# One PSUM tile per bank, another start order and filler matmuls in a fused attention and channel-mix kernel

## The chip, the cores and the metric

The kernel runs on one core of a Trainium2 chip. The metric is the device time of one execution in microseconds (us), lower is better. A profile is one execution, taken beside the timed ones. PE is the matrix engine, ACT the scalar engine, DVE the vector engine, POOL is GpSimd, SP the sync engine.

## The reference

Eight batches, eight heads, 576 positions, head size 64. Linear attention comes first, then a channel mix with d_model 512 and d_ff 1024:

```
q_s = softmax(q over d);  k_s = softmax(k over positions)
x   = q_s @ (k_s^T @ v)              # per batch and head, then heads side by side: [8, 576, 512]
xk  = mu_k*x + (1-mu_k)*x_prev       # x_prev is x, one position earlier
xr  = mu_r*x + (1-mu_r)*x_prev
out = sigmoid(xr @ w_r) * (relu(xk @ w_k)^2 @ w_v)
```

## The kernel before

The kernel plans itself. It lists operations with an estimated length, a sort key and dependencies, orders them in a small simulation, and writes the instructions in that order. Each engine then runs its own list strictly in order and waits on semaphores. The semaphores are not set by the planner but by the framework, from the tiles that the instructions read and write.

PSUM has eight banks of 128 x 512 f32. The kernel before takes them as four tiles of two banks. The planner, however, hands out six slots: two pairs ("att") and four single banks ("mm"):

```python
banks = [psum.tile([128, 2, 512], F32, name=f"bank_{x}") for x in "abcd"]
ps = {"mm": [banks[2 + i // 2][:, i % 2, :] for i in range(4)],
      "att": [t[:, :, :] for t in banks[0:2]], "early": [t[:, :, :] for t in banks[2:4]]}
```

So mm slots 0 and 1 are the two halves of tile bank_c, and slots 2 and 3 those of bank_d. The steady work is in units of 512 columns. Each unit has 8 wk groups, and for each 128 columns an r group and two v groups, all in mm slots (four 512-column matmuls each):

```python
# K: 4 matmuls into a mm slot, then ACT relu, then DVE square -> k2
# R: 4 matmuls into a mm slot, then ACT tanh -> th
# V: 8 matmuls (two groups of 4) into a mm slot, then DVE (th + 1) * v -> ot, then a store
# ... (cut)
o = plan.add("PE", 0.864, 1.03, clock, lambda v=v_part: v(range(4, 8)),
             squares[4:8] + [o] + wv_done[1:2], [], [k2])
```

The data of a V group come from DVE (the squares) and from wv, never from ACT.

The start: batch 0's q, k, v come on the SP and ACT queues, weights and all other batches on POOL's queue. Batch 0 is mixed on PE with masked weights built from mu:

```python
gate = [first[GATE]]                 # the first wk load waits for one of batch 0's loads
# ... (cut)
mask_zeros = plan.add("POOL", 2.2, 2.3, -7, emit_mask_zeros)
# mu_rows: two loads on ACT's queue per mu; mask copies: 4 DVE instructions per mu
```

The softmax here doesn't subtract the row's maximum and nothing guards it: scores larger than these inputs give would overflow.

## Time and profile before

| | before |
|---|---|
| median of 3 runs | 230.28 us |
| span of the profiled execution | 228.7 us |
| first transposes of q | 11.49 us |
| first wk matmul | 22.63 us |
| unit 1's first r matmul | 60.16 us |
| last matmul ends | 224.07 us |

The page's lines for span and busy time of each engine:

```profile
span 228.7 us, 3591 instructions
PE 196.1 (86%) x1281; PEld 98.1 (43%) x1281; DVE 164.9 (72%) x368; ACT 152.3 (67%) x228; POOL 41.6 (18%) x65
```

PE is the busiest engine. Its columns alone, at the steady rate of 0.86 us for four 512-column matmuls, come to about 190 us, so roughly 38 us of the span are not PE work. The timeline of the first 24 us shows one part. Its columns are start, length, engine, line, operation, output<-input, shapes, count, and in brackets the idle time before it and its releaser:

```profile
5.75 1.25 ACT L399 ACTIVATE eq_a<-raw_a 128x576 bf16<-128x576 f32 x2 [1.23 <-DMA raw_a<-in_q_dram]
8.44 1.42 DVE L413 TENSOR_REDUCE rsum_a<-eq_a 128x9 f32<-128x576 bf16 x2
...
11.49 1.14 PE L443 MATMUL bank_a<-ident,qs_a 128*128 128x128 bf16 x9 [2.75 <-DVE qs_a L421]
...
16.30 1.17 PE L496 MATMUL bank_a<-qt_a,wp_a 128*128 128x512 bf16 x5
...
22.63 1.44 PE L617 MATMUL bank_c<-xk,wk_bf 128*128 128x512 bf16 x4
...
23.91 0.66 PE L496 MATMUL bank_b<-qt_a,wp_b 128*128 128x512 bf16 x5
```

PE waits 11 us for a chain load, exp, row sum, scale. The same five mixing matmuls take 1.17 us at 16.30 and 0.66 us at 23.91, so PE runs at half rate until about then. Below, "cold" means matmuls at this half rate and "warm" at the full one, always read from their lengths.

The other part is spread over the steady stretch. The view of waits lists what ended PE's idle time there (releaser: us in total, times, longest); these are five of its eight lines for 60 to 120 us:

```profile
PE bank_d L617 <- DVE ot_c L664: 1.2, 1, 1.2
PE bank_c L658 <- ACT th_b L653: 1.0, 1, 1.0
PE bank_d L617 <- ACT rel_b L602: 0.8, 1, 0.8
PE bank_d L617 <- ACT rel_a L602: 0.7, 1, 0.7
PE bank_d L658 <- ACT rel_a L602: 0.7, 1, 0.7
```

From 60 us to the end such lines add to 8.4 us in 15 waits (the view lists waits above 0.15 us). They look like ordinary waits for a free PSUM slot. The second one is not, and the timeline around it shows why (L648 is an r group, L658 a v group, th_b a tanh):

```profile
86.48 1.03 PE L648 MATMUL bank_c<-wr_bf,xr 128*128 128x512 bf16 x4
87.34 1.03 PE L658 MATMUL bank_d<-wv_bf,k_a 128*128 128x512 bf16 x4
88.72 0.61 ACT L653 ACTIVATE th_b<-bank_c 128x512 f32<-128x512 f32 x1
...
89.38 1.02 PE L658 MATMUL bank_c<-wv_bf,k_a 128*128 128x512 bf16 x4 [1.02 <-ACT th_b L653]
```

The r group at 86.48 fills one half of bank_c. ACT reads it with th_b only at 88.72, having been busy. The v group that follows wants the other half of bank_c, which nobody uses, and still waits until the tanh is done.

### The profile page before, as it was taken

What the parts mean: (1) busy time and instruction counts of PE and PEld (TensorE: products, weight loads), DVE (VectorE), ACT (ScalarE), POOL (GpSimd) and SP (SyncE); (2) the same over time, 40 slices, a digit from 0 to 9 for tenths busy, and PEclk for the clock granted to TensorE, in tenths of its full rate; (3) what the DMA queues carried; (4) which work ended last, traced back from release to release, by engine and by line L of the source; (5) the groups of instructions that cost most, each with busy time, mean ns of one, the idle gap of its engine ahead of it and who ended that gap; (6) DMA issues with size and microseconds to landing.
All of it is one profiled execution on the core that took longest, in us unless ns stands there. A gap on an engine that the chain in (4) does not pass through costs nothing. (4 is left out here: it accounts for less than half of the span.)

```text
span 228.7 us, 3591 instructions
## 1 busy us (share of the span) xinstructions
PE 196.1 (86%) x1281; PEld 98.1 (43%) x1281; DVE 164.9 (72%) x368; ACT 152.3 (67%) x228; POOL 41.6 (18%) x65
## 2 busy tenths in 40 slices
PE   0076999967899878998979999999999999999881
PEld 0053444533354434543446544444543454444530
DVE  1774855898899959989787989699578538832521
ACT  2658689798898688587427897957775664452430
POOL 8615437344322122112000000000000000000000
PEclk9999999999999999999999999999999999999999
DMA  6999999999999858868372040222042122403404
GB/s 199 299 292 357 209 338 390 402 399 402 393 400 404 290 193 232 237 159 268 109 195 46 4 92 0 64 63 62 0 94 67 25 49 46 92 0 91 94 3 92
DMA packets 16722, 40.88 MB, mean 179 GB/s; under 512 B 2360, under 2 KB 5184, under 8 KB 16704
## 3 DMA queue, kind: packets, MB, share of 16 engines
q0 software_dynamic: 8896, 27.40, 37.3%
q1 hardware_dynamic: 7200, 12.39, 20.1%
q10 hardware_dynamic: 608, 0.85, 1.2%
q8 instruction: 10, 0.16, 0.3%
q14 instruction: 8, 0.07, 0.1%
HBM read 33.82 MB, written 9.44 MB: 189 GB/s over the span
## 5 line engine op out<-in xcount | busy, mean ns | idle before, releaser
L617 PEld LDWEIGHTS <-wk_bf 128*128 128x128 bf16 x320 | 30.6, 98 | 39.0 <-issue 9.9
L617 PE MATMUL bank_d<-xk,wk_bf 128*128 128x512 bf16 (+1 forms) x160 | 37.1, 357 | 3.5 <-DVE ot_c L664 1.2
L617 PE MATMUL bank_c<-xk,wk_bf 128*128 128x512 bf16 (+1 forms) x160 | 37.6, 360 | 2.3 <-ACT rel_a L602 1.6
L658 PEld LDWEIGHTS <-k_a 128*128 128x128 bf16 x144 | 13.5, 97 | 18.9 <-issue 3.0
L658 PE MATMUL bank_c<-wv_bf,k_a 128*128 128x512 bf16 x80 | 20.2, 379 | 1.3 <-ACT th_b L653 1.0
L658 PEld LDWEIGHTS <-k_b 128*128 128x128 bf16 x144 | 13.5, 97 | 17.5 <-issue 3.1
L648 PEld LDWEIGHTS <-xr 128*128 128x128 bf16 x144 | 13.3, 98 | 17.3 <-issue 2.4
L658 PE MATMUL bank_d<-wv_bf,k_b 128*128 128x512 bf16 x80 | 20.2, 379 | 0.3 <-DVE ot_b L664 0.3
L648 PE MATMUL bank_c<-wr_bf,xr 128*128 128x512 bf16 x72 | 18.5, 379 | 0.8 <-ACT rel_c L602 0.6
L648 PE MATMUL bank_d<-wr_bf,xr 128*128 128x512 bf16 x72 | 18.5, 379 | 0.5 <-ACT th_b L653 0.5
L658 PE MATMUL bank_d<-wv_bf,k_a 128*128 128x512 bf16 x64 | 16.1, 379 | 1.6 <-DVE ot_c L664 0.9
L658 PE MATMUL bank_c<-wv_bf,k_b 128*128 128x512 bf16 x64 | 16.2, 379 | 1.2 <-DVE ot_b L664 0.8
L602 ACT ACTIVATE rel_c<-bank_d 128x512 bf16<-128x512 f32 (+1 forms) x17 | 9.3, 547 | 8.7 <-PE bank_d L617 8.1
L602 ACT ACTIVATE rel_b<-bank_c 128x512 bf16<-128x512 f32 (+1 forms) x17 | 9.5, 559 | 5.9 <-PE bank_c L617 5.2
L653 ACT ACTIVATE th_a<-bank_c 128x512 f32<-128x512 f32 x10 | 6.0, 598 | 7.3 <-PE bank_c L648 3.4
L602 ACT ACTIVATE rel_a<-bank_c 128x512 bf16<-128x512 f32 (+1 forms) x14 | 7.5, 539 | 4.0 <-PE bank_c L617 3.8
L653 ACT ACTIVATE th_a<-bank_d 128x512 f32<-128x512 f32 x8 | 4.8, 599 | 6.4 <-PE bank_d L648 5.7
L602 ACT ACTIVATE rel_a<-bank_d 128x512 bf16<-128x512 f32 (+1 forms) x13 | 7.4, 570 | 1.8 <-PE bank_d L617 1.6
L606 DVE TENSOR_TENSOR k_a<-rel_b 128x512 bf16<-128x512 bf16 (+1 forms) x14 | 5.6, 404 | 3.9 <-ACT rel_b L602 3.7
L443 PE MATMUL bank_a<-ident,qs_a 128*128 128x128 bf16 x72 | 5.8, 230 | 2.8 <-DVE qs_a L421 2.8
L447 ACT COPY qt_a<-bank_a 128x1152 bf16<-128x1152 bf16 x5 | 5.6, 1117 | 3.7 <-PE bank_a L443 3.7
L653 ACT ACTIVATE th_b<-bank_c 128x512 f32<-128x512 f32 x8 | 4.8, 598 | 4.8 <-PE bank_c L648 4.5
(208 smaller groups left out, 389.0 us busy)
## 6 DMA issues: line engine op xcount, KB each, us to landing
out_dram<-ot_a SPq DMA_DIRECT2D x24, 128.0 KB, 2.4
out_dram<-ot_b SPq DMA_DIRECT2D x24, 128.0 KB, 2.4
out_dram<-ot_c SPq DMA_DIRECT2D x24, 128.0 KB, 2.4
raw_a<-in_q_dram POOLq DMA_DIRECT2D x3, 576.0 KB, 8.7
raw_b<-in_q_dram POOLq DMA_DIRECT2D x3, 576.0 KB, 7.0
raw_c<-in_k_dram POOLq DMA_DIRECT2D x3, 576.0 KB, 7.7
raw_d<-in_v_dram POOLq DMA_DIRECT2D x3, 576.0 KB, 8.5
raw_e<-in_k_dram POOLq DMA_DIRECT2D x3, 576.0 KB, 9.7
```

What stands on the lines that cost most here:

```text
L443: nc.tensor.transpose(out=transposed()[:, j, :], in_=qss[qs.index][:, j, :], identity=ident[:])
L447: nc.scalar.copy(out=qts[qt.index][:], in_=transposed()[:, 0:J, :])
L602: nc.scalar.activation(out=rels[rel.index][:, 0:n], in_=bank(kf)[:, 0:n], func=ACT.Relu, scale=HALF_ROOT)
L606: nc.vector.tensor_tensor(out=k2s[k2.index][:, fc, 0:n], in0=rels[rel.index][:, 0:n], in1=rels[rel.index][:, 0:n], op=ALU.mult)
L617: nc.tensor.matmul(bank(kf)[:, 0:n], lhsT=wk_bf[:, ct, fc * 128:(fc + 1) * 128], rhs=xs[0][:, ct, c0:c0 + n], start=(ct == 0), stop=(ct == ...
L648: nc.tensor.matmul(bank(rps), lhsT=xs[1][:, ct, c:c + 128], rhs=wr_bf[:, ct, :], start=(ct == 0), stop=(ct == CT - 1))
L653: nc.scalar.activation(out=ths[th.index][:], in_=bank(rps), func=ACT.Tanh, scale=0.5)
L658: nc.tensor.matmul(bank(vps), lhsT=k2s[k2.index][:, ft, 128 * m:128 * m + 128], rhs=wv_bf[:, ft, :], start=(ft == 0), stop=(ft == FT - 1))
```

## The change

The intent is to take false waits out of PSUM and to shorten the start. The PSUM part, with `kv_of` picking the single bank where the first batch's k^T v used a pair:

```diff
-    banks = [psum.tile([128, 2, 512], F32, name=f"bank_{x}") for x in "abcd"]
-    ps = {"mm": [banks[2 + i // 2][:, i % 2, :] for i in range(4)],
-          "att": [t[:, :, :] for t in banks[0:2]], "early": [t[:, :, :] for t in banks[2:4]]}
+    ps = {"mm": [psum.tile([128, 512], F32, name=f"mm_{x}") for x in "abcd"],
+          "att": [psum.tile([128, 2, 512], F32, name=f"att_{x}") for x in "ab"]}
+    def kv_of(slot, hf):
+        if slot.pool == "early":
+            return ps["mm"][2 * slot.index + hf][:]
+        return bank(slot)[:, hf, :]
```

The start part, cut to its core:

```diff
-                if closed:
+                if closed and not op.size:          # loads keep the order they are given
-    mask_zeros = plan.add("POOL", 2.2, 2.3, -7, emit_mask_zeros)      (on GpSimd)
+    mask_zeros = plan.add("DVE", 1.8, 1.9, 0, emit_mask_zeros)        (on DVE)
-            nc.scalar.dma_start(            # mu_rows
+            nc.gpsimd.dma_start(
-            nc.vector.tensor_copy(out=mu_mask...); nc.vector.tensor_scalar(...)
+            nc.gpsimd.tensor_copy(out=mu_mask...); nc.gpsimd.tensor_scalar(...)
+    def filler(slot):
+        for _ in range(2):
+            nc.tensor.matmul(bank(slot)[:, 0:128], lhsT=ident[:], rhs=ident[:], start=True,
+                             stop=True)
+    for _ in range(FILL):                   # FILL = 40
+        slot = Slot("mm")
+        plan.add("PE", 0.11, 0.2, 2 * LATE, lambda slot=slot: filler(slot), [identity], [slot],
+                 [slot])
(cut: some lengths and keys that the planner uses, and a reciprocal split in two)
```

The first line has a consequence that the diff hides: batch 0 now loads as q, q, k, v, and the gate of the weights, unchanged in the text, now falls on the v of the first head group, the last of its loads. In the kernel before that v was issued first, so the gate opened at once.

More of the change, by code (lines that the diff above doesn't have):

```diff
@@ L34 @@
 GATE = 7
-MU_KEY = (0.5, 1.9, LATE, LATE)
+FILL = 40
 ON_PE = (0,)
@@ L233 @@
     ots = buffers("ot", [128, C], F32)
-    banks = [psum.tile([128, 2, 512], F32, name=f"bank_{x}") for x in "abcd"]
-    ps = {"mm": [banks[2 + i // 2][:, i % 2, :] for i in range(4)],
-          "att": [t[:, :, :] for t in banks[0:2]], "early": [t[:, :, :] for t in banks[2:4]]}
+    ps = {"mm": [psum.tile([128, 512], F32, name=f"mm_{x}") for x in "abcd"],
+          "att": [psum.tile([128, 2, 512], F32, name=f"att_{x}") for x in "ab"]}
     def bank(slot):
-        return ps[slot.pool][slot.index]
+        return ps[slot.pool][slot.index][:]
+    def kv_of(slot, hf):
+        if slot.pool == "early":
+            return ps["mm"][2 * slot.index + hf][:]
+        return bank(slot)[:, hf, :]
     xs = [const.tile([128, CT, RING], BF16, name=n) for n in ("xk", "xr")]
@@ L300, in emit_mask_zeros @@
     def emit_mask_zeros():
-        nc.gpsimd.memset(mu_mask[:].rearrange("p m s c e -> p (m s c e)"), 0.0)
+        nc.vector.memset(mu_mask[:].rearrange("p m s c e -> p (m s c e)"), 0.0)
     def emit_late_consts():
@@ L310 @@
     plan.add("ACT", 2.0, 2.0, 1.5, emit_warm, [zero])
-    mu_load = plan.add("POOL", 1.2, 1.2, -9, emit_mu_load, size=8.0)
-    identity = plan.add("POOL", 0.6, 0.8, -8, emit_identity)
-    consts = plan.add("DVE", 0.5, 0.6, -9, emit_consts, [identity])
+    mu_load = plan.add("POOL", 1.2, 1.2, -9.2, emit_mu_load, size=8.0)
+    identity = plan.add("POOL", 0.6, 0.8, -9.1, emit_identity)
+    consts = plan.add("DVE", 0.2, 0.3, -9, emit_consts, [identity])
     late_consts = plan.add("DVE", 0.6, 0.7, LATE, emit_late_consts)
-    mask_zeros = plan.add("POOL", 2.2, 2.3, -7, emit_mask_zeros)
+    mask_zeros = plan.add("DVE", 1.8, 1.9, 0, emit_mask_zeros)
     mu_slot = Slot("mm")
@@ L335, in emit_mu_mask @@
             r = slice(64 * u, 64 * u + 64)
-            nc.vector.tensor_copy(out=mu_mask[r, m, 0, :, r], in_=mu_rows[r, m, :, :])
-            nc.vector.tensor_scalar(out=mu_mask[r, m, 1, :, r], in0=mu_rows[r, m, :, :],
+            nc.gpsimd.tensor_copy(out=mu_mask[r, m, 0, :, r], in_=mu_rows[r, m, :, :])
+            nc.gpsimd.tensor_scalar(out=mu_mask[r, m, 1, :, r], in0=mu_rows[r, m, :, :],
                                     scalar1=-1.0, scalar2=1.0, op0=ALU.mult, op1=ALU.add)
     mu_t = plan.add("PE", 0.2, 0.4, -500, emit_mu, [mu_load, consts], [mu_slot])
-    mu_done = plan.add("DVE", 0.08, 0.17, LATE, emit_mu_copy, [mu_t], gives=[mu_slot])
+    mu_done = plan.add("DVE", 0.08, 0.17, 0, emit_mu_copy, [mu_t], gives=[mu_slot])
     mu_masked = []
     for m in range(2):
-        o = plan.add("ACT", 0.9, 0.9, MU_KEY[m], lambda m=m: emit_mu_rows_load(m), size=131.0)
-        mu_masked.append(plan.add("DVE", 1.0, 1.1, MU_KEY[2 + m], lambda m=m: emit_mu_mask(m),
+        o = plan.add("POOL", 1.4, 1.4, -9.5 + m, lambda m=m: emit_mu_rows_load(m), size=131.0)
+        mu_masked.append(plan.add("POOL", 1.6, 1.7, -2 + m, lambda m=m: emit_mu_mask(m),
                                   [o, mask_zeros]))
+    def filler(slot):
[6 more added lines that the diff above has]
+                 [slot])
     def weight_part(dst, src, n, u, c0, c1):
@@ L429, in kv @@
                     nc.tensor.matmul(
-                        bank(kvp)[:, hf, 0:129],
+                        kv_of(kvp, hf)[:, 0:129],
                         lhsT=eks[ek.index][r, j, :, :].rearrange("p u d -> p (u d)"),
@@ L434, in recz @@
         def recz():
-            nc.vector.reciprocal(out=rzs[rz.index][:, :, None],
-                                 in_=bank(kvp)[:, :, 128:129])
+            if kvp.pool == "att":
+                nc.vector.reciprocal(out=rzs[rz.index][:, :, None],
+                                     in_=bank(kvp)[:, :, 128:129])
+            else:
+                for hf in range(2):
+                    nc.vector.reciprocal(out=rzs[rz.index][:, hf:hf + 1],
+                                         in_=kv_of(kvp, hf)[:, 128:129])
         def transposed():
@@ L480, in attention @@
         kvm = plan.add("PE", 0.63, 0.7, pe_key, kv, expk + castv, [kvp], [ek, vv])
-        zdone = plan.add("DVE", 0.066, 0.15, step + 2, recz, [kvm], [rz])
+        zdone = plan.add("DVE", 0.08 * (2 if b == 0 else 1), 0.25 if b == 0 else 0.16, step + 2, recz, [kvm], [rz])
         def weights_of(wp, m, hf, s):
             nc.vector.scalar_tensor_tensor(
-                out=wps[wp.index][:, hf, s, :], in0=bank(kvp)[:, hf, 0:128],
+                out=wps[wp.index][:, hf, s, :], in0=kv_of(kvp, hf)[:, 0:128],
                 scalar=rzs[rz.index][:, hf:hf + 1], in1=mu_mask[:, m, s, 2 * g + hf, :],
@@ L571, in attention @@
                                 [xb] if hf == 0 else [], [xps[hf]]))
-        o = plan.add("DVE", 0.1, 0.19, step + 6, edge, evs)
+        o = plan.add("DVE", 0.11, 0.19, step + 6, edge, evs)
         xdiff = plan.add("DVE", 0.66, 0.755, step + 6, diff, [o], [xd])
```

## The prediction

> **What bounds the kernel now.** The page gives PE 86% busy, ACT 67%, DVE 72%. At the warm rate of the steady stretch (0.86 us per four 512-column matmuls, start to start) PE's columns need about 190 us of the 228.7 us span. The timeline shows where the other 38 us are. (a) Start: only one tiny transpose runs on PE until 11.49 us, and the first wk matmul starts at 22.63; under 4 us of warm-equivalent work is done by then, so about 19 us are lost. (b) The last matmul ends at 224.1; gate and store take 4.6 us. (c) About 14 us between, in waits of 0.2 to 1.3 us with an ACT or DVE reader of a bank as releaser ("th_b", "rel_a", "ot_c").
>
> The start is a latency chain. v is loaded first and the weights start at 4.66 us, before batch 0 is in. The first exp waits for q until 5.75, DVE's mu masks push the first row sum to 8.44, group 1's k and v compete with weights (last v cast at 19.38), and PE is cold: five mixing matmuls take 1.17 us until 22 us and 0.66 from 23.9. The granted-clock row shows 9 throughout and hides this; the Trainium skill, "TensorE: Matmul & The Clock Gate", section "What's actually happening", states that an idle array runs at half rate until about 3.4 us of sustained activity, which the factor here fits.
>
> **What the change does.**
> - Load order q, k, v and a weight gate on group 0's last v (about 9 us, from 362 GB/s in 2.5 to 5 us): first exp about 4.6.
> - Masks to GpSimd, their zeroing to DVE (1.8 us while DVE idles): first row sum about 5.4, first transposes about 8.7.
> - Group 0's kv about 10.5 (was 14.27), group 1's about 14 (21.54).
> - 80 filler matmuls: cold about 0.11 us each, warm half; they end at 7.5 to 9 us, delay nothing and leave PE warm, worth about 0.5 us for each of some five groups, 2 us.
> - First wk half lands about 16; first wk matmul about 17.5, with more mixing already done: PE about 6 us ahead.
> - One tile per bank: in the old program v matmuls wait for ACT though their data come only from DVE, i.e. for the tanh or relu reading the other bank of a two-bank tile. After 60 us about 8 us of listed PE waits name such readers; I expect 2 to 3 us back.
>
> **What takes some back.** Weights and batch 1 move the same bytes through a saturated DMA (share over 1.0 from 7.5 to 60 us), so wv's second half still lands near 32.5 and PE will wait 1 to 2 us there; ACT and DVE are nearly full (DVE 18.1 of 20 us in 40 to 60). So about 5 us of the start survive, plus 2 to 3.
>
> **Prediction.** 223 us (80%: 219.5 to 226.5). Faster by over 2%: 0.85; within 2%: 0.14; slower: 0.01.
>
> **What would show it.** Timeline: fillers from 1.5 to about 8 us, mixing groups at 0.66 us before 15 us, first wk matmul at 16 to 18.5. Waits: DMA wv releasing PE near 32 us; th/ot/rel releasers of PE after 60 us roughly halved. PE's last matmul about 7 us earlier.
>
> **What would make it wrong.** Slow GpSimd masks delay wk's issue, queued behind them; gaps after the fillers let PE cool; the reordered program puts new ACT/DVE waits between 40 and 80 us that return the gain; or per-bank tiles bring more than 3 us.

## The result, and the profile after

The changed kernel takes 215.24 us (median of 4 runs, 214.19 to 216.73) against 230.83 us (4 runs of before). The ratio is 0.9329, with a 95% interval of 0.9255 to 0.9403. Ratios here are the mean time of one kernel's runs over the mean of the other's of the same rounds, so they are not quite the ratio of the medians. The gain is 15.6 us; 7.8 us were predicted, with a range down to 219.5 us.

| | before | after |
|---|---|---|
| span of the profiled execution | 228.7 | 212.6 |
| first transposes of q | 11.49 | 8.24 |
| first wk matmul | 22.63 | 19.93 |
| unit 1's first r matmul | 60.16 | 55.94 |
| last matmul ends | 224.07 | 207.80 |
| from unit 1's first r to the last matmul | 163.9 | 151.9 |

The page of the changed kernel:

```profile
span 212.6 us, 3757 instructions
PE 197.4 (93%) x1361; PEld 103.6 (49%) x1361; DVE 163.3 (77%) x363; ACT 151.4 (71%) x228; POOL 44.8 (21%) x76
```

The start, as the timeline has it (L354 fillers, L462 transposes, L515 mixing, L636 wk):

```profile
1.37 0.39 PE L354 MATMUL mm_a<-ident 128*128 128x128 bf16 x2 [1.37 <-POOL ident masks.py:199]
4.48 1.26 ACT L413 ACTIVATE eq_a<-raw_a 128x576 bf16<-128x576 f32 x2 [1.31 <-DMA raw_a<-in_q_dram]
5.19 1.41 DVE L427 TENSOR_REDUCE rsum_a<-eq_a 128x9 f32<-128x576 bf16 x2 [1.63 <-ACT eq_a L413]
...
8.24 0.68 PE L462 MATMUL att_a<-ident,qs_a 128*128 128x128 bf16 x9
...
13.39 1.14 PE L515 MATMUL att_a<-qt_a,wp_a 128*128 128x512 bf16 x5
...
19.93 0.60 PE L636 MATMUL mm_c<-xk,wk_bf 128*128 128x512 bf16 x2
```

Exp, row sum and transposes come 1.3, 3.3 and 3.3 us sooner. But mixing at 13.39 us runs at half rate again (1.14 us), and the first wk matmul is only 2.7 us sooner.

Busy time by stretch (start:end, length, then busy us and count for PE, PEld, DVE, ACT, POOL, then granted clock, DMA share, GB/s), before and then after:

```profile
60.00:120.00 60.00, 54.41 (x341) 26.48 (x340) 52.15 (x103) 43.38 (x61) 11.28 (x16) 1.00 0.80 256
120.00:180.00 60.00, 58.74 (x391) 29.46 (x389) 49.04 (x110) 45.06 (x68) 0.00 (x0) 1.00 0.22 49
```

```profile
60.00:120.00 60.00, 60.00 (x434) 31.60 (x433) 56.53 (x121) 48.79 (x72) 11.87 (x17) 1.00 0.77 265
120.00:180.00 60.00, 60.00 (x406) 29.36 (x404) 48.01 (x107) 44.57 (x65) 0.00 (x0) 1.00 0.25 61
```

From 60 us on PE has no idle time in the changed kernel: the view of waits is empty for PE there. All that is left after 20 us stands in four lines before 52 us:

```profile
PE mm_c L636 <- DVE xk L579: 2.2, 1, 2.2
PE mm_c L636 <- ACT rel_c L621: 1.6, 1, 1.6
PE att_a L515 <- ACT xr L520: 0.8, 1, 0.8
PE mm_a L677 <- DMA wv_bf<-in_moe_w_v_dram: 0.8, 2, 0.4
```

So the stretch after unit 1's first r matmul gave 12.0 us and the part ahead of it 4.2 us. About 1 us of that split is order, not speed: the old order does two k^T v groups of batch 2 (about 0.5 us each) ahead of that point, the new one behind it. So the 12.0 is about 1 us too small and the 4.2 as much too large. The experiments ask which part of the change did what.

### The profile page after: what moved, and what is told of

Its sections match the earlier page's. It is cut to its first block, busy times and chain, and to the rows that moved or that the text cites. A ratio compares the mean times of both kernels' runs of the same rounds, so it can differ in the third digit from the quotient of the medians.

```text
span 212.6 us, 3757 instructions
## 1 busy us (share of the span) xinstructions
PE 197.4 (93%) x1361; PEld 103.6 (49%) x1361; DVE 163.3 (77%) x363; ACT 151.4 (71%) x228; POOL 44.8 (21%) x76
## 4 chain that ended last, share of the span: by engine, by line
PE 73%; DMA 18%; POOL 2%; ACT 2%; issue 1%; SPq 1%; DVE 0%; POOLq 0%; DVEq 0%
PE mm_a L677 7%; PE mm_c L636 7%; PE mm_a L636 7%; PE mm_c L677 7%; PE mm_d L677 7%; PE mm_d L636 6%; PE mm_b L677 6%; DMA raw_j<-in_q_dram 5%; PE mm_b L636 5%; PE mm_b L667 4%; DMA raw_d<-in_q_dram 4%; DMA wk_bf<-in_moe_w_k_dram 4%; PE mm_d L667 4%; DMA raw_d<-in_v_dram 4%; PE mm_c L667 2%; PE mm_a L667 2%
## 5 line engine op out<-in xcount | busy, mean ns | idle before, releaser
L636 PEld LDWEIGHTS <-wk_bf 128*128 128x128 bf16 x320 | 30.7, 98 | 35.8 <-issue 5.5
L636 PE MATMUL mm_c<-xk,wk_bf 128*128 128x512 bf16 (+1 forms) x92 | 22.3, 356 | 3.9 <-DVE xk L579 2.2
L636 PE MATMUL mm_a<-xk,wk_bf 128*128 128x512 bf16 (+1 forms) x88 | 21.3, 355 | 0.0
L677 PEld LDWEIGHTS <-k_b 128*128 128x128 bf16 x144 | 13.3, 98 | 15.2
L667 PEld LDWEIGHTS <-xr 128*128 128x128 bf16 x144 | 13.3, 98 | 15.2
L636 PE MATMUL mm_d<-xk,wk_bf 128*128 128x512 bf16 (+1 forms) x76 | 18.5, 357 | 0.1
L636 PE MATMUL mm_b<-xk,wk_bf 128*128 128x512 bf16 (+1 forms) x64 | 15.9, 366 | 0.0
L677 PE MATMUL mm_a<-wv_bf,k_a 128*128 128x512 bf16 x48 | 12.3, 379 | 0.8 <-DMA wv_bf<-in_moe_w_v_dram 0.8
L677 PE MATMUL mm_c<-wv_bf,k_b 128*128 128x512 bf16 x48 | 12.3, 379 | 0.0
L667 PE MATMUL mm_b<-wr_bf,xr 128*128 128x512 bf16 x44 | 11.3, 379 | 0.0
L667 PE MATMUL mm_d<-wr_bf,xr 128*128 128x512 bf16 x40 | 10.3, 380 | 0.0
L677 PE MATMUL mm_d<-wv_bf,k_a 128*128 128x512 bf16 x40 | 10.3, 379 | 0.0
L677 PE MATMUL mm_b<-wv_bf,k_a 128*128 128x512 bf16 x40 | 10.1, 380 | 0.0
## 6 DMA issues: line engine op xcount, KB each, us to landing
raw_a<-in_q_dram POOLq DMA_DIRECT2D x2, 576.0 KB, 10.3
```

The costliest lines, as they stand in the source:

```text
L636: nc.tensor.matmul(bank(kf)[:, 0:n], lhsT=wk_bf[:, ct, fc * 128:(fc + 1) * 128], rhs=xs[0][:, ct, c0:c0 + n], start=(ct == 0), stop=(ct == ...
L667: nc.tensor.matmul(bank(rps), lhsT=xs[1][:, ct, c:c + 128], rhs=wr_bf[:, ct, :], start=(ct == 0), stop=(ct == CT - 1))
L677: nc.tensor.matmul(bank(vps), lhsT=k2s[k2.index][:, ft, 128 * m:128 * m + 128], rhs=wv_bf[:, ft, :], start=(ft == 0), stop=(ft == FT - 1))
```

## The experiments

All kernels gave correct results. Each call to the chip ran its own executions of the kernel before, 228 to 232 us; ratios are to those. "After" means the changed kernel; it was run again as a yardstick.

### Yardsticks: the changed kernel again (a1, a2, a3)

> The changed kernel once more, as the yardstick on this chip for the runs beside it: 214 to 217 us, no PE wait listed after 60 us.

> The changed kernel once more, yardstick on this chip for the three runs beside it: 213.5 to 216 us.

> The changed kernel once more, yardstick on this chip: 213.5 to 216.5 us; profiles so far had matmuls at half rate somewhere in 48 to 56 us in some executions and not in others.

Measured: 214.50, 215.56 and 214.01 us; ratios 0.9287, 0.9352 and 0.9267. So the same kernel, in medians of six runs, lies within 1.6 us from call to call. Differences of under about 1 us between single kernels are not resolved here. a1's expectation of no PE wait after 60 us was off in the letter: its profile lists two waits of 0.2 us in the class "issue", that is, with no releaser.

### e1: one tile per bank, and nothing else

```diff
 (kernel before)
-    banks = [psum.tile([128, 2, 512], ...) for x in "abcd"]; ps = {"mm": halves of banks c and d, ...}
+    ps = {"mm": [psum.tile([128, 512], F32, ...) for x in "abcd"], "att": two tiles of two banks}
```

PE, ACT, POOL and SP have the same instructions in the same order as before; DVE has two reciprocals split in two.

> The kernel before with one PSUM tile per bank and nothing else; the program order of every engine is unchanged except that two reciprocals are split in two. Theory A (PE's gaps after 60 us in the kernel before, 13.8 us of start-to-start excess, are waits for a reader of the other bank of a two-bank tile): about 218 to 220 us, PE gaps after 60 us under 3 us, start unchanged (first wk matmul 22 to 23 us). Rival B (the gaps went because the plan put the instructions in another order): 229 to 231 us with the th/rel/ot releasers of PE still there.

Measured: 215.32 us, ratio 0.9328 (0.9296 to 0.9360). That is below what theory A expected and equal to the whole change within the scatter. The first wk matmul is at 21.95 us, unit 1's first r matmul at 57.96 (60.16 before), and from there to PE's end it takes 150.6 us (163.9). So 13.3 us come from behind unit 1's first r matmul and 2.2 from ahead of it; the order is the same in both kernels, so no shift of work is in these numbers. From there to the end, e1's view of waits on PE has two lines left, and neither names a reader:

```profile
PE mm_b L657 <- issue: 0.2, 1, 0.2
PE mm_c L657 <- issue: 0.2, 1, 0.2
```

Rival B, the new order, is out as the cause of the gain. Whether each old wait was false in itself, or some only passed on the delay of an earlier one, was not separated.

The place shown above looks like this in e1, where the program order is the same (the r group now fills mm_a, the v groups mm_c and mm_b):

```profile
81.43 1.03 PE L657 MATMUL mm_a<-wr_bf,xr 128*128 128x512 bf16 x4
...
82.30 1.03 PE L667 MATMUL mm_c<-wv_bf,k_a 128*128 128x512 bf16 x4
...
82.81 0.61 ACT L662 ACTIVATE th_b<-mm_a 128x512 f32<-128x512 f32 x1
83.16 1.03 PE L667 MATMUL mm_b<-wv_bf,k_a 128*128 128x512 bf16 x4
```

The tanh reads mm_a until 83.42; the v group into mm_b starts at 83.16, in the middle of it, and waits for nothing.

### e2: the changed kernel with the two-bank tiles back

```diff
 (changed kernel)
-    ps = {"mm": [psum.tile([128, 512], F32, ...) for x in "abcd"], ...}
+    banks = [psum.tile([128, 2, 512], ...) for x in "abcd"]; ps = {"mm": halves of banks c and d, ...}
```

> The changed kernel with the two-bank tiles put back; order of every engine unchanged except the two split reciprocals, which are joined again. Theory A (tiles carry the gain): 13 to 15 us are lost again, 227 to 230 us, and ACT and DVE readers release PE all through 60 to 220 us. Rival (the start's changes carry a part that the tiles hid, so the parts overlap): 220 to 225 us. Rival B (the new order carries it): about 215 us.

Measured: 227.16 us, ratio 0.9882 (0.9822 to 0.9943). Theory A holds. Some of the releasers of PE that come back:

```profile
PE bank_c L627 <- DVE ot_a L674: 1.0, 3, 0.5
PE bank_c L668 <- ACT th_b L663: 0.9, 2, 0.7
PE bank_d L668 <- DVE ot_c L674: 0.9, 1, 0.9
```

The four kernels form a square. With the two-bank tiles, the start's changes are worth 1.2%, about 2.7 us by the ratio. With one tile per bank, e1 at 0.9328 stands against 0.9329, 0.9287, 0.9352 and 0.9267 for the changed kernel, a mean of 0.9309: about 0.4 us by the mean and 0.9 us against the changed kernel (a1, 0.9287), not resolved. The parts overlap; no run shows which waits they share.

### e5: four banks in one tile

```diff
 (kernel before)
-    banks = four tiles of two banks
+    banks = two tiles of two banks (att);  quad = psum.tile([128, 4, 512], F32, name="quad")
+    ps = {"mm": [quad[:, i, :] for i in range(4)], "early": halves of quad, ...}
```

> The kernel before with all four single banks in one tile instead of two tiles of two banks; order of every engine unchanged. Theory A (waits follow tiles, not banks) wants more false waits: slower than the kernel before by at least 6 us, 236 to 260 us. If the cost came from two engines meeting in the chip's banks and not from waits that the program sets, the banks used are the same and it stays at 229 to 232 us.

Measured: 325.17 us (322.71 to 329.65), ratio 1.4118. The order of every engine is that of the kernel before, and so is the number of banks; only the tile is larger. The direction is what theory A expects, the size is far over its range. The profile fell on a slow run, so only the kind of its waits is used here, and that is the same kind:

```profile
PE quad L619 <- ACT rel_a L604: 13.9, 18, 1.5
PE quad L660 <- ACT th_b L655: 8.8, 13, 0.9
PE quad L619 <- DVE ot_c L666: 4.1, 5, 0.8
```

With one, two and four mm banks per tile the kernel before takes 215.3, 230.6 and 325.2 us. That the chip itself makes engines queue for a bank is no explanation. The Trainium skill, "PSUM — Partial Sum Buffer", section "PSUM bank collisions raise a hardware error", states that the hardware neither arbitrates nor stalls there and that a kernel has to guard by bank with semaphores. The runs agree in so far as 94.6 us more appear with a change of tile alone, and the waits end on ACT and DVE instructions.

### e3 and e3b: no fillers

```diff
 (changed kernel)
-        for _ in range(2):
+        for _ in range(0):      # planned, not emitted: all else keeps its place
```

> The changed kernel with the 80 filler matmuls planned but not emitted, so every other instruction keeps its place. Theory A (PE cooled again at about 12.9 us in the changed kernel, so the fillers only made the first transposes and the first kv group warm): 0 to 1 us slower than the changed kernel, mixing at 1.14 us in both. Rival C (the fillers are what brings the start forward): 2 to 4 us slower, first wk matmul after 22 us.

> The kernel of e3 (fillers planned but not emitted) a second time, because the profile of e3 fell in its fastest run and showed no loss while its median was 1.9 us over the changed kernel's. If the fillers do pay: again 1.5 to 2 us slower than the changed kernel, and a profile of a typical run shows PE cold beyond 20 us. If that was chance: within 0.7 us of it.

Measured: e3 216.44 us, ratio 0.9365 against 0.9287 for the changed kernel; e3b 214.96 us, 0.9332 against 0.9352. The first would say that fillers are worth 1.8 us, the second that they are worth nothing. Within e3's call the two intervals do not overlap (0.9330 to 0.9400 against 0.9252 to 0.9323), so e3 alone would have been read as a loss. That it was scatter is inferred from the repeat, and from e11 below. The first wk matmul comes at 19.52 and 18.93 us, within or ahead of the range of the four profiles of the changed kernel (19.16 to 20.40 us). Rival C, with 2 to 4 us and a first wk matmul after 22 us, is out; a gain of up to about 1 us cannot be excluded.

### e4: fillers that bridge the gap in which PE cooled

```diff
 (changed kernel)
+    bridge(14)      # 28 identity matmuls behind the mu transpose
+    bridge(8)       # 16 behind the first transposes of q
```

> The changed kernel with 8 more pairs of fillers after the first transposes and 14 after the mu transpose, to bridge the 3 us in which PE cooled. If warmth lasts, the mixing groups from 13 us take 0.66 instead of 1.14 us and the first wk matmul comes at about 18.8 us (19.9) where the first half of wk lands. Theory D (after that the loads of batch 1 and ACT set the pace until 52 us): whole kernel within 0.7 us of the changed one. Rival C (cold PE is what the start is limited by): 1.5 to 3 us faster.

Measured: 214.47 us, ratio 0.9288 (changed kernel 0.9287). The warmth did last: mixing took 0.68 us at 13.22, and the first wk matmul came at 18.81 us, 1.1 us sooner than in the profile of the result. Nothing of it reached the end. The second half of unit 1's first wk group, the line with the 2.2 us wait, started at 48.37 us against 48.54:

```profile
48.37 0.59 PE L644 MATMUL mm_c<-xk,wk_bf 128*128 128x512 bf16 x2 [2.28 <-DVE xk L587]
```

That the bridge kept PE warm is not shown by this one profile: e9 below has no bridge and mixed at 0.68 us too (13.15 us). The four profiles of the changed kernel say the same of the start: a1 has the latest first wk matmul of them (20.40 us) and the earliest start of that line (47.61 us). Theory D holds on this point: PE's speed in the first 20 us is not what the start is limited by.

### e6: tiles and fillers, on the old start

```diff
 (e1)
+        for i in range(120):    # ahead of everything else on PE
+            nc.tensor.matmul(ps["mm"][i // 2 % 4][:, 0:128], lhsT=ident[:], rhs=ident[:], ...)
```

> The kernel before with one tile per bank and 60 pairs of fillers ahead of everything on PE, old load order, old masks. If the fillers alone are worth the 1.9 us that the run without them lost, 213 to 214 us, about 1.8 us under the run with tiles alone. If they only pay with the new load order, 215 to 215.8 us.

Measured: 215.95 us, ratio 0.939 (0.9342 to 0.9438); e1 0.9328. It was run at another time. The fillers bring no gain here. In the profile they end at about 10.2 us and the first transposes run warm (0.68 us), but k^T v starts only at 15.55 us, behind a wait of 3.48 us for v, and mixing is at half rate again (1.12 us).

### e7: weights released earlier

```diff
 (changed kernel)
-GATE = 7
+GATE = 3                        # batch 0's q is in, instead of its first v
-        ... "POOL", 1.6, 1.7, -2 + m, emit_mu_mask
+        ... "POOL", 1.6, 1.7, 1.1 + 0.01 * m, emit_mu_mask
```

> The changed kernel with the weights released when batch 0's q is in instead of its first v, and the first mask copies behind wk on GpSimd; only GpSimd's order moves. If holding the weights is what put batch 1's loads 3 us back (the last v of batch 1 landed near 40 us against 37) and that is where the start's gain went: loads of batch 1 land 2 to 3 us sooner, ACT no longer waits for q of batch 1 near 36 us, 212.5 to 213.5 us. If the weights then only take bandwidth from batch 0: 214 to 216 us, with the first v cast later than 10.3 us.

Measured: 215.26 us, ratio 0.936 (0.9315 to 0.9405); no gain. wk was issued from 6.39 us on (11.44 in the changed kernel), and ACT's wait of 1.87 us for batch 1's q near 36 us did go. But batch 0's second v arrived late: its last cast started at 17.40 us, and the first wk matmul at 23.16. Both sides of the expectation were half right; the first v cast, at 9.94 us, was not later than 10.3. The order of the loads moves the wait from one batch to the other.

### e8: a megabyte more ahead of batch 1

```diff
 (changed kernel)
+        if h == 1:
+            nc.gpsimd.dma_start(out=spare[:], in_=ap)     # half of wv once more, nobody reads it
```

> The changed kernel with the second half of wv read once more into a tile that nobody uses (1.05 MB more, queued ahead of batch 1's second head group); no other instruction moves. Theory D (the loads up to batch 1 set when the second half of unit 1's wk matmuls can start, 48.5 us in the changed kernel): that point and the whole kernel move by 2 to 3 us, to 216.5 to 218 us. Rival (ACT and DVE set it, the loads have slack): under 1 us, 214 to 215.5 us.

Measured: 216.86 us, ratio 0.9441 against 0.9352 for the changed kernel: 0.89% of 230.8 us, 2.1 us. The start of the second half of unit 1's first wk group, called the 48 us mark from here on, in the profile of the changed kernel and in that of e8:

```profile
48.54 0.59 PE L636 MATMUL mm_c<-xk,wk_bf 128*128 128x512 bf16 x2 [2.25 <-DVE xk L579]
```

```profile
50.84 0.59 PE L639 MATMUL mm_c<-xk,wk_bf 128*128 128x512 bf16 x2 [2.39 <-DVE xk L582]
```

In all four profiles of the changed kernel this mark lies at 47.61 to 48.54 us; in e8 2.3 us behind the latest of them, with 4.13 us of ACT waiting for batch 1's q. Theory D holds: the bytes up to batch 1's second head group set the pace of the start. The intervals of the two ratios overlap a little (0.9378 to 0.9504, 0.9300 to 0.9405), so the mark carries this and the total supports it.

### e9: masks ahead of the weights

```diff
 (changed kernel)
-        ... lambda m=m: emit_mu_mask(m)
+        ... lambda m=m: [emit_mu_mask(i) for i in range(2) if m == 0]
```

> The changed kernel with all mask copies on GpSimd ahead of wk, so that they no longer sit between wk and batch 1's loads (1.6 us of GpSimd at 14 to 15.6 us); only GpSimd's order moves. Theory D: batch 1's loads issue and land 1 to 1.5 us sooner, the kernel gets 0.5 to 1.2 us faster (213 to 214 us). If the DMA engines were full over that stretch anyway: within 0.3 us of the changed kernel.

Measured: 215.29 us, ratio 0.9381 (changed kernel 0.9352); no gain. The masks then delayed wk itself from 11.44 to 12.65 us, and batch 1's q was still issued at 24.63 (24.67). GpSimd's place for the masks is not what holds the loads.

### e10 and e11: fillers in the two waits near 46 to 51 us

Some profiles of nearly identical kernels had PE at half rate behind those two waits. This is yardstick a2, its row of the timeline and its stretches; the granted clock is the third number from the end:

```profile
51.42 1.01 PE L636 MATMUL mm_c<-xk,wk_bf 128*128 128x512 bf16 x2 [0.93 <-ACT rel_c L621]
...
53.08 1.06 PE L636 MATMUL mm_c<-xk,wk_bf 128*128 128x512 bf16 x2
```

```profile
50.00:52.00 2.00, 1.07 (x4) 0.27 (x3) 2.00 (x4) 2.00 (x4) 0.71 (x1) 0.50 1.05 418
52.00:54.00 2.00, 2.00 (x7) 0.65 (x5) 1.94 (x3) 1.38 (x2) 0.87 (x2) 0.50 1.05 400
```

A group of two takes 0.59 us when warm. In a2 and e4 unit 1's first r matmul came at 58.02 and 58.21 us, though the mark at 48 us was where it is elsewhere; in the profile of the result it came at 55.94. a2 is the same program as that one, so 2 us of this is scatter between executions. Being cold there need not cost so much: in a1 PE was at half rate from 47.61 to about 50.6 us and the r matmul came at 55.08 us, with a wait for rel_c behind it of 0.31 us instead of 1.57.

```diff
 (changed kernel; e11: the same without the fillers at the start)
+            if (half, c0) == (0, 512):
+                calls[0] += 1
+                for _ in range({4: 36, 7: 22}.get(calls[0], 0)):
+                    nc.tensor.matmul(ps["att"][0][:, 0, 0:128], lhsT=ident[:], rhs=ident[:], ...)
```

> The changed kernel with 36 filler matmuls ahead of the second half of unit 1's first wk matmuls and 22 ahead of the next wait, both of which PE spends idle (2.3 and 1.6 us at 45.7 to 51.5 us). Theory F (cooling in those two waits is where about 2 us go in some executions, and why a start that is ahead gains little on the median): clock 1.00 in all of 45 to 60 us, first r matmul of unit 1 at 55 to 56 us, median about 213.5 us, 0.7 to 1.5 us under the yardstick, with less spread. If cooling there does not matter: equal to the yardstick within 0.4 us.

> The same middle fillers, but the 80 fillers at the start planned and not emitted. If the start's fillers are worth nothing where the loads set the pace: equal to the run with both within 0.4 us. If they are: 1 us or more slower.

Measured: a3 214.01, e10 213.69, e11 213.91 us; ratios 0.9267, 0.9265 and 0.9275. The waits are filled and the clock stays at 1.00 in the profiles of e10 and e11, but it also did in a3, whose six runs all lie in 213.39 to 214.28 us. So on this chip there was nothing to mend, and e10 and e11 each had one run over 215 us all the same. Whether the middle fillers help where PE does cool is not shown. e11 equals e10, which supports that the fillers at the start are worth nothing that can be measured here.

## Why the prediction was right or wrong

The direction and the chance of a gain were right, and so was the mechanism of the tiles. "Per-bank tiles bring more than 3 us" stands among the things that the prediction said would make it wrong, and that is what happened. The time was 4.3 us below the low end of the range, and the split between the parts was wrong in both terms.

**The step that failed: "After 60 us about 8 us of listed PE waits name such readers; I expect 2 to 3 us back."** The cause was named correctly; the term was mis-sized. e1, the tiles alone, gives 15.4 us by the medians, of which 13.3 lie behind unit 1's first r matmul. Two errors are in it. First, all of the listed waits went, not a third. For this discount the prediction gives no reason but that "ACT and DVE are nearly full", so that they would take the gain back. They did not: in the changed kernel DVE is busy for 56.53 of the 60 us from 60 to 120 us (52.15 before) and PE has no wait there. Second, the list is a lower bound. A wait is counted from the modelled end of the last matmul, and a group of four is shown as 1.03 us long though the next one starts 0.86 us after it when nothing stalls. So each wait hides about 0.17 us. An estimate from the trace: 8.4 us listed and 15 times 0.17 us hidden make about 11 us. Counted in the trace as the time from one matmul's start to the next beyond the steady spacing, these 15 waits cost 10.8 us, and another 18 delays of 0.06 to 0.30 us each, of which the list shows none, add 2.8 us. Together that is 13.6 us, against the 13.3 us that e1 gained there.

**"So about 5 us of the start survive": mis-sized the other way.** With two-bank tiles the start's changes are worth about 2.7 us (e2), with one tile per bank 0.4 to 0.9 us, which is not resolved. The steps of the chain were nearly right: first exp 4.48 us (4.6 predicted), row sum 5.19 (5.4), transposes 8.24 (8.7), group 0's k^T v 11.90 (10.5), group 1's 15.21 (14), the last filler at 7.9 us. But the chain was not what bound the stage. Unit 1 needs batch 1, and batch 1's second head group comes after all of batch 0 and all weights on DMA engines that are full (a DMA share of 1.0 or more in every stretch from 2.5 to 60 us of the changed kernel). The prediction said that batch 1 and the weights share a full DMA, but drew the consequence for wv only (1 to 2 us) and left the wait for batch 1 out. e8 shows that more bytes move the 48 us mark, e4 that a warmer and earlier PE does not, e7 and e9 that reordering the loads does not bring the end forward.

**Fillers: "delay nothing and leave PE warm, worth ... 2 us".** They delayed nothing and warmed PE; the filler pairs start 0.21 us apart up to about 5.8 us and 0.11 us apart after. But PE was idle for most of 9 to 11.9 us and mixing ran at half rate at 13.39 us, where 0.66 us was predicted before 15 us. The prediction named this among the things that would make it wrong. Warm in e4, it still gained nothing.

**The weights' gate.** It was expected to open near 9 us and wk's first half to land near 16. It opened at 11.44 us, and the two loads of that half landed at 16.28 and 18.47 us. In the profile of the result the first wk matmul came 1.5 us later still (19.93 us, 16 to 18.5 predicted), without a wait of its own, straight behind mixing groups at half rate.

Right: waits of PE for wv (at 32.49 and 35.38 us, 0.8 us in total; 1 to 2 predicted near 32), mask copies on GpSimd that cost little (0.39 to 0.61 us each).

What stays open: why the two parts overlap by about 2 us; how much of the scatter of the changed kernel is cooling near 50 us; and whether the fillers are worth anything under 1 us.

## What to carry to other kernels

Where the framework derives waits from tiles, a tile that holds two independently used PSUM banks makes its users wait for each other, and no plan of slots undoes it: make tiles as small as what is reused alone. In a trace, ask of each wait whether the waiting instruction needs anything that its releaser made or freed; where it does not, count the whole wait as gain, and add the pipeline's drain; here 8.4 us of listed waits stood for 13.3 us. A start that is faster on the critical engine gains only up to the next thing that the loads set, so follow the bytes up to the first point where that engine never waits again.

## What the Trainium skill lacked or had wrong

- No page says that a program's waits can follow the tile and not the bank. "PSUM — Partial Sum Buffer" gives the rule to guard by bank; it does not say what a coarser guard costs. Here: 215.3, 230.6 and 325.2 us with one, two and four banks per tile.
- "TensorE: Matmul & The Clock Gate", section "What's actually happening", gives a return to half rate after at least one idle window of about 3.4 us. Here a2's PE was back at half rate at 49.4 us behind a single wait of 2.25 us with matmuls on both sides, and the profile of the result, with the same wait of 2.25 us, stayed at full rate. The rates in the same page's section "Wait — 56ns, not 53.3ns?" agree: filler pairs 0.21 us apart cold and 0.11 us warm are 107 and 56 ns a matmul, as the table there has them.
- The same page, section "Seeing it yourself", warns that clock events in a trace can be unreliable, but does not name this form: in the kernel before the granted clock reads 1.00 from the start, while five mixing matmuls take 1.17 us at 16.30 us and 0.66 at 23.91; in the changed kernel it reads 0.50 to 0.58 from 12.5 to 20 us for the same thing. Matmul lengths, not the clock row, showed PE cold at the start.
